# Fused attention and two expert layers on one core: the second raw copy and the gate rows of each head move forward, and 16 products of the first expert move ahead of its last columns

## The chip, the cores and the metric

The kernel runs on one core of a Trainium2 chip. The metric is the device time of one execution in microseconds (us), median over the runs. The kernel before was timed three times: 811.89, 816.52 and 813.16 us, median 813.16 us. The execution that the profiler recorded took 811.05 us.

## What is computed

Attention with a decaying causal mask over 4 batches of 8 heads, 576 positions and 64 channels a head, then two layers of experts on the 2304 rows that come out:

```python
scores = scale * np.matmul(q, k.transpose(0, 1, 3, 2))
cum = np.cumsum(np.log(np.clip(f, 0.0001, 1.0)), axis=-1)
scores = np.where(causal, -1e9, scores + cum[..., :, None] - cum[..., None, :])
attn = np.exp(scores - scores.max(-1, keepdims=True))
attn = attn / (attn.sum(-1, keepdims=True) + 1e-9)
x = (attn @ v).transpose(0, 2, 1, 3).reshape(2304, 512)
...
# layer 1: each row goes to the expert of its largest normalised logit
out[mask] = gate_w[mask, None] * (np.maximum(x[mask] @ w1[e], 0) @ w2[e])
...
# layer 2: each expert takes exactly 288 rows, in the order of the logits
out[mask] = np.maximum(x[mask] @ w1[e], 0) @ w2[e]
```

There are 8 experts in each layer, with 1024 hidden columns.

## The kernel before, in words

The 32 heads (4 batches by 8) are worked off in 32 slots; one slot takes some 7 us in the trace. Everything in a slot is written in a fixed order by hand, and each engine carries out its own instructions in that order, so an instruction that waits holds all that stands behind it on its engine. Products are kept at float32 precision by splitting each operand into a rounded high part and the remainder.

For head n there are two operand tiles: `opA` (the high parts, with rows for the mask, the row maximum and the gate sums below them) and `opB` (the remainders, crosswise). Three buffers of each go round, so slot n prepares head n+2 in the buffers that head n-1 has used. A preparation has these pieces:

- `load(n + 3)`: the raw q and k of a head that is one further on come from memory into `raw` (L307), and every second time v transposed into `vt` (L314). `load2(n + 2)`: two rows of gate sums go from `chl` into rows 64 and 65 of `opA` (L462, 2.2 KB each) and v by rows into `vv` (L463). All of these are asked for on the queue of SP.
- `prep(n + 2)` (L465) has two halves, t = 0 for q and t = 1 for k. Each half is a ScalarE (ACT) copy of `raw` into `opA` (L469), a GpSimd (POOL) subtraction that gives the remainder in `opB` (L470), and a request on SP that copies the high part across to the other half of `opB` (L471). Half 0 is issued at step 0 of the slot and half 1 at step 4.

The slot has six steps, the loop over i in L743. Step i issues one pair of score products of head n on TensorE (PE) with their exponentials on ACT (`st_steps`, L544 to L546, into PSUM tiles `px`), one product for the row maxima of head n+1 (`max_steps`, L508, into two PSUM tiles `pl`, reduced on VectorE (DVE) in L512 and L516), and some of the products of head n-1 with v (`av_steps`, L577). At i = 3 POOL splits the maxima (`rows1`, L523). After the six steps PE transposes the maxima (`rows`, L528), ACT puts them into `opA` (L529), and the first two maxima products of head n+2 are issued, mixed with the remaining products of L577. The first of those is the first reader of half 1 of the preparation and of the gate rows:

```python
nc.tensor.matmul(p[:, :wp], af[0:96, q0:q0 + 128], a[0:96, 1, k0:k0 + wp], start=True, stop=True)
```

Behind the last slot the routing of the rows to experts is computed, mostly on DVE, while PE already works on the first expert with the 256 rows that were known early: 96 products of 256 columns, 12 for each of 8 pieces of the hidden layer (`First.products`, L967). `fill(n)` issues the next n of them, and the seven numbers in `FILL` say how many go where. The last 112 rows of this expert come by an indirect transfer into `tail` (L947); `First.columns` turns them (four transposes on PE in L883, copies on ACT in L886, remainders on DVE in L887). Pieces 6 and 7 use the fourth part of the weights, whose high part `whi` is made on ACT and whose remainder `wlo` is made on DVE by `split(3)` (L812, then L857 and L863), behind the ordering of the experts (`order_all`, L162). Then `Experts.run` goes on with the last rows (L1567).

```python
first_expert.fill(FILL[3] - FILL[6])
first_expert.rest()
first_expert.fill(FILL[5])
first_expert.columns()
first_expert.fill(96 - sum(FILL[:4]) - FILL[5])
```

`rest` (L985) issues six subtractions on POOL (L990).

Of the kernel before, what the change touches and what calls it, by code (L numbers as in the profile page):

```python
# [25 lines left out]
N = B * S  # L26
# [12 lines left out]
AHEAD = (4, 5)  # L39
LATE = (0, 1, 2, 3)  # L40
BESIDE = (0, 0, 0, 0, 1, 2, 3, 2, 2)
FILL = (11, 9, 16, 36, 4, 0, 12)
EARLY = 256

TAILS1 = {0: (0, 0), 1: (1, 0), 2: (2, 0), 3: (2, 64), 4: (3, 0), 5: (3, 64), 6: (3, 96)}
# [6 lines left out]
def r32(ap):  # L52
    return ap.bitcast(F32)
# [236 lines left out]
def attention(tc, ctx, qkT, vrow, vT, f, emb, x_d, identf, identb, psum, R, tau, first_expert):  # L290


    nc = tc.nc
# [23 lines left out]
    def load(n):  # L317
        load_raw(n)
        load_vt(n)
# [17 lines left out]
    low = const.tile([128, 1], F32, name="low")  # L337
    nc.gpsimd.iota(low, pattern=[[0, 1]], base=64, channel_multiplier=-1, allow_small_or_imprecise_dtypes=True)

    NB = 3  # L340
# [4 lines left out]
    Ab, Bb = ([t[:, 0:2 * S].rearrange("p (t s) -> p t s", t=2) for t in ts] for ts in (Af, Bf))  # L345
# [5 lines left out]
    chl = const.tile([B * H, 2, S], F32R, name="chl")  # L351
# [5 lines left out]
    def ln(t):  # L357
        nc.scalar.activation(t, t, AF.Ln)
# [40 lines left out]
    def weights_of(k):  # L399


        t = R.room(k, [128, NCH * S + 64], F32)
        pt = t[:, 0:NCH * S].rearrange("p (j s) -> p j s", j=NCH)
        nc.gpsimd.memset(pt[:, 1:, 0:64], 1.0)
        nc.gpsimd.memset(t[:, NCH * S:], 1.0)
        nc.gpsimd.memset(pt[64:128, NCH - 1, S - 64:], 0.0)
        return t, pt
# [48 lines left out]
        for k in range(2):  # L456
            nc.vector.tensor_tensor(ENB[:, :, k + 1], ENB[:, :, k], half(ENB[:, :, k]), op=ALU.subtract)

    def load2(n):
        b, h = divmod(n, H)  # L460
        for i in range(2 if n > 1 else 0):
            nc.sync.dma_start(r32(Ab[n % NB][64 + i:65 + i, 1, :]), r32(chl[n:n + 1, i, :]))  # L462
        nc.sync.dma_start(Vb[n % 4][:, :, 0:D], vrow[b, h])  # L463

    def prep(n):  # L465
        a, b_, raw = Ab[n % NB], Bb[n % NB], RAW.pop(n)

        def half(t, hi, lo):
            nc.scalar.activation(a[0:64, t, :], raw[:, t, :], AF.Copy)  # L469
            nc.gpsimd.tensor_tensor(b_[lo, t, :], raw[:, t, :], r32(a[0:64, t, :]), op=ALU.subtract)  # L470
            nc.sync.dma_start(r32(b_[hi, t, :]), r32(a[0:64, t, :]))  # L471
        top, low = slice(0, 64), slice(64, 128)
        return [lambda: half(0, low, top), lambda: half(1, top, low)]

    def parts(n):

        v, r = VT[n][:, 0:S], cum0[:, n // 2 % 2, 0:S]
        (nc.vector if n else nc.gpsimd).tensor_tensor(r, v, half(v), op=ALU.subtract)
        yield
        (nc.gpsimd if n > 2 else nc.vector).tensor_tensor(half(r, 0), r, half(r), op=ALU.subtract)  # L480
# [39 lines left out]
    def rows1(n):  # L520

        mx = MB[n % 2][:, :, 48:49]
        nc.gpsimd.tensor_tensor(half(mx, 0), mx, half(mx), op=ALU.subtract)  # L523
# [7 lines left out]
    def st_steps(n):  # L531
        a, b_, af, bf = Ab[n % NB], Bb[n % NB], Af[n % NB], Bf[n % NB]
        pt = PT[n % 2][1]
        out = []
        for j, q0, q1 in ((0, 0, 288), (0, 288, 576), (1, 128, 576), (2, 256, 576), (3, 384, 576),
                          (4, 512, 576)):
            def step(j=j, q0=q0, q1=q1):
                kw = min(128, S - j * 128)
                k0 = j * 128
                w = q1 - q0  # L540
                wp = w if w <= 64 else max(w, 256)
                p = psum.tile([128, 512], F32, name="px", bufs=3)
                o, ks = p[:, 512 - wp:], slice(S + k0, S + k0 + 128)
                nc.tensor.matmul(o, af[:, ks], a[:, 0, q1 - wp:q1], start=True, stop=False)  # L544
                nc.tensor.matmul(o, bf[:, ks], b_[:, 0, q1 - wp:q1], start=False, stop=True)
                nc.scalar.activation(pt[:kw, j, q0:q1], p[:kw, 512 - w:], AF.Exp, scale=0.125)  # L546
                if j in (1, 3):
                    fl = pt.rearrange("p j s -> p (j s)")
                    d = bass.AP(tensor=fl.tensor, offset=fl.offset + (j - 1) * (S + 128),
                                ap=[fl.ap[0], [S + 128, 2], [1, 128]])  # L550
                    nc.gpsimd.affine_select(d, d, pattern=[[0, 2], [1, 128]], compare_op=ALU.is_ge,
                                            fill=0.0, base=0, channel_multiplier=-1)
                elif j == 4:
                    nc.gpsimd.affine_select(pt[:64, 4, 512:576], pt[:64, 4, 512:576],
                                            pattern=[[1, 64]], compare_op=ALU.is_ge,
                                            fill=0.0, base=0, channel_multiplier=-1)
            out.append(step)
        return out
# [3 lines left out]
    def av_steps(n):  # L562
        b, h = divmod(n, H)
        v_ = Vb[n % 4]
        p = AV[n % 2]
        if h == 0 and b not in X:
            X[b] = (work.tile([128, NCH, DM], F32, name="xr"),
                    work.tile([128, NCH, E, H], F32, name="lh"))
        out = []
        seen = []  # L570
        for i in AORD:
            j = seen.count(i)
            seen.append(i)

            def step(i=i, j=j, k=len(seen) - 1):
                c = j * S + i * 128
                nc.tensor.matmul(p[:, i, :], PT[n % 2][0][:, c:c + 128], v_[:, j, :], start=(k == 0),  # L577
                                 stop=(k == len(AORD) - 1))
            out.append(step)
        return out  # L580
# [110 lines left out]
    N = B * H  # L691
    for s in prep(0):
        s()
    second()
    pads()
    PT = [weights_of("hh")]
    load2(0)
    load2(1)
    ln(fr)
    h1 = prep(1)  # L700
    un = unit()
    next(un)
# [24 lines left out]
    def emit(l, k):  # L727
        for _ in range(k):
            if l:
                l.pop(0)()  # L730
    fin = iter(())
    pa = []
    for n in range(N):
        if n + 3 < N:
            load(n + 3)
        if n + 2 < N:
            load2(n + 2)
        pp = prep(n + 2) if n + 2 < N else []
        ss = st_steps(n)
        aa = av_steps(n - 1) if n else []  # L740
        if n % 2 == 0 and n + 2 < N:
            pa.append(parts(n + 2))
        for i in range(6):  # L743
            emit(ss, 1)
            emit(ms, 1)
            if n == 0 and i == 2:
                unit_columns()
            if n == 0 and i == 5:
                warm(nc, psum, identb, START[4], "px", 3)
            if i == (3 if n else 5) and n + 1 < N:  # L750
                rows1(n + 1)
                next(p0, None)
            if i in (0, 4):
                emit(pp, 1)
            emit(aa, APAT[i])
            if i in (1, 2):
                next(fin, None)
            if i in VPAT[min(n, 2 + n % 2)]:
                advance(pa, 1)
            if i in NPAT:  # L760
                advance(now, 1)
            if i in QPAT:
                advance(sq or slow, 1)
            if i in FPAT:
                advance(first3, 1)
            if i == 3:
                store()
        if n + 1 < N:
            rows(n + 1)
        ms = max_steps(n + 2) if n + 2 < N else []  # L770
        emit(ms, 1)
        emit(aa, 1)
        emit(ms, 1)
        emit(aa, 15)
        if (n % 2 or not n) and n + 1 < N:
            ven(n + n % 2)
        if n == 0:
            warm(nc, psum, identb, START[5], "px", 3)
        if n:
            fin = av_fin(n - 1)  # L780
            next(fin)
        if n == 1:
            now.append(setup())
# [7 lines left out]
    first_expert.W.upper(0, 2)  # L791
    first_expert.fill(FILL[0])
    for _ in av_fin(N - 1):
# [3 lines left out]
    for _ in range(2):  # L797
        first_expert.load_next()
    first_expert.fill(FILL[1])
    advance(sq, FILL[4])  # L800
    advance(now, 100)
    R.total = carry[0]
    first_expert.fill(FILL[2])
    u = R.tokens(psum, "px", 3, NC1, *R.one_hots)
# [8 lines left out]
    first_expert.load_next()  # L813
    first_expert.fill(FILL[6])
    advance(sq, 100)
    first_expert.fill(FILL[3] - FILL[6])
    first_expert.rest()
# [7 lines left out]
N = B * S  # L825
# [13 lines left out]
class Weights:  # L839
# [13 lines left out]
    def upper(self, key, j):  # L853
        pool, k, bufs = (self.pool, "1", 4) if j < 4 else (self.pool2, "2", 8)
        hi = pool.tile([128, 1024], F32R, name="whi" + k, bufs=bufs)
        lo = pool.tile([128, 1024], F32R, name="wlo" + k, bufs=bufs)
        self.nc.scalar.activation(hi, self.raw[key, j], AF.Copy)  # L857
        self.parts[key, j] = (hi, lo)

    def lower(self, key, j):  # L860

        hi, lo = self.parts[key, j]
        self.nc.vector.tensor_tensor(lo, self.raw.pop((key, j)), r32(hi), op=ALU.subtract)  # L863
# [1033 lines left out]
```

## Time and profile before

| what | before |
| --- | --- |
| median of three runs | 813.16 us |
| the profiled execution | 811.05 us |
| its span in the profile | 809.3 us |
| PE busy with products, share of the span | 741.2 us, 92% |
| PE busy with weight loads | 707.5 us, 87% |
| DVE busy | 500.6 us, 62% |
| ACT busy | 408.6 us, 50% |
| POOL busy | 302.6 us, 37% |

The span is the time from the first to the last instruction that the profiler recorded; the execution's own time is 1.75 us longer. Times in the rows further down are counted from the span's start. Slot 0 begins at about 29.5 us and the last slot ends at about 257 us; the first expert's last columns fall at about 271 us.

### The profile page before, as it was taken

How to read it: one execution, taken by the hardware profiler on the slowest of the kernel's cores; microseconds unless marked ns; L12 is line 12 of the kernel's file. 1: busy time of each engine (PE TensorE's matmuls, PEld its weight loads, DVE VectorE, ACT ScalarE, POOL GpSimd, SP SyncE). 2: the span in 40 equal slices, each digit the busy share in tenths (PEclk: the TensorE clock that was granted, in tenths of full speed). 3: DMA queues.
4: the chain of work that ended last, by engine and by line, in shares of the span. 5: the costliest groups of instructions: out<-in, count | busy, mean ns of one | idle time of the engine just before them, and what ended most of it. 6: DMA issues, size and time to landing. Idle time of an engine off the chain costs nothing. (4 is left out here: it accounts for less than half of the span.)

```text
span 809.3 us, 16361 instructions
## 1 busy us (share of the span) xinstructions
PE 741.2 (92%) x5813; PEld 707.5 (87%) x5813; DVE 500.6 (62%) x1314; ACT 408.6 (50%) x898; POOL 302.6 (37%) x674
## 2 busy tenths in 40 slices
PE   3799999999999899999999999925799999999995
PEld 1499999999989899999999999822799999999993
DVE  5766786787786777465465567674555655555530
ACT  3455666666756645455465567100555545555420
POOL 5676767676661635621222111003012322232011
PEclk9999999999999999999999999855899999999998
DMA  5455656566545456555566663004556656665310
GB/s 123 95 131 140 164 134 173 143 151 154 153 114 199 142 182 215 169 177 163 163 174 201 196 184 108 16 12 152 178 176 187 205 181 197 208 187 180 125 36 30
DMA packets 70255, 121.75 MB, mean 150 GB/s; under 512 B 29498, under 2 KB 38714, under 8 KB 70164
## 3 DMA queue, kind: packets, MB, share of 16 engines
q1 hardware_dynamic: 63924, 101.24, 44.3%
q0 software_dynamic: 6240, 19.36, 6.4%
q8 instruction: 50, 0.82, 0.4%
q14 instruction: 41, 0.34, 0.1%
HBM read 96.46 MB, written 14.63 MB: 137 GB/s over the span
## 5 line engine op out<-in xcount | busy, mean ns | idle before, releaser
L863 DVE TENSOR_TENSOR wlo<-wraw,whi 128x1024 fp32r<-128x1024 f32 x128 | 156.4, 1227 | 126.3 <-ACT whi L857 122.0
L857 ACT ACTIVATE whi<-wraw 128x1024 fp32r<-128x1024 f32 x128 | 134.6, 1056 | 4.3 <-DMA wraw<-v 3.5
L470 POOL TENSOR_TENSOR opB<-raw,opA 64x576 fp32r<-64x576 f32 x64 | 90.5, 1415 | 44.2 <-ACT opA L469 38.1
L1570 ACT ACTIVATE room_hh<-pl 128x288 fp32r<-128x288 f32 (+8 forms) x128 | 51.9, 406 | 96.9 <-PE pl L1567 96.4
L1567 PE MATMUL pl<-room_xh,whi 128*128 128x288 f32 (+7 forms) x512 | 94.7, 307 | 4.6 <-DVE room_hl L1571 4.4
L1567 PE MATMUL pl<-room_xl,whi 128*128 128x288 f32 (+7 forms) x512 | 90.5, 299 | 0.0
L1567 PE MATMUL pl<-room_xh,wlo 128*128 128x288 f32 (+7 forms) x512 | 90.0, 298 | 0.0
L1591 PE MATMUL py<-room_hh,wlo 128*128 128x288 f32 (+7 forms) x480 | 89.8, 311 | 0.0
L1571 DVE SCALAR_TENSOR_TENSOR room_hl<-pl,room_hh 128x288 fp32r<-128x288 f32 (+8 forms) x128 | 57.2, 448 | 50.5 <-ACT room_hh L1570 50.2
L1567 PEld LDWEIGHTS pl<-room_xh,whi 128*128 128x128 f32 x512 | 76.0, 191 | 6.3 <-DVE room_hl L1571 5.9
L508 PE MATMUL pl<-opA 96*128 96x288 f32 (+2 forms) x192 | 67.8, 358 | 11.2 <-DVE opA L382 4.4
L1567 PEld LDWEIGHTS pl<-room_xl,whi 128*128 128x128 f32 x512 | 76.7, 191 | 0.1
L1567 PEld LDWEIGHTS pl<-room_xh,wlo 128*128 128x128 f32 x512 | 76.2, 190 | 0.0
L1591 PE MATMUL py<-room_hh,whi 128*128 128x288 f32 (+7 forms) x480 | 76.0, 301 | 0.0
L1591 PE MATMUL py<-room_hl,whi 128*128 128x288 f32 (+7 forms) x480 | 75.8, 300 | 0.0
L1799 POOL DMA_INDIRECT xg<-y_d,ix x24 | 29.2, 1215 | 123.4 <-PE px L1507 88.5
L544 PE MATMUL px<-opA 128*128 128x288 f32 (+2 forms) x192 | 71.8, 374 | 0.1
L1591 PEld LDWEIGHTS py<-room_hh,wlo 128*128 128x128 f32 x480 | 70.6, 190 | 0.0
L577 PE MATMUL py<-vv,room_hh 128*128 128x73 f32 x480 | 69.8, 265 | 0.4 <-DVE vv L492 0.4
L512 DVE CUSTOM_DVE_ANT_0 mxs<-pl,mask 128x512 f32<-128x512 f32 (+3 forms) x128 | 61.9, 484 | 12.6 <-PE pl L508 9.1
L1591 PEld LDWEIGHTS py<-room_hh,whi 128*128 128x128 f32 x480 | 69.1, 189 | 0.0
L1591 PEld LDWEIGHTS py<-room_hl,whi 128*128 128x128 f32 x480 | 69.0, 189 | 0.0
(367 smaller groups left out, 1410.8 us busy)
## 6 DMA issues: line engine op xcount, KB each, us to landing
wraw<-w SPq DMA_DIRECT2D x64, 512.0 KB, 3.6
wraw<-v SPq DMA_DIRECT2D x64, 512.0 KB, 3.5
raw<-qkT SPq DMA_DIRECT2D x32, 288.0 KB, 4.1
opB<-opA SPq DMA_DIRECT2D x64, 144.0 KB, 2.7
vv<-vrow SPq DMA_DIRECT2D x32, 160.0 KB, 3.3
vt<-vT SPq DMA_DIRECT2D x16, 288.0 KB, 4.4
x_d<-xr SPq DMA_DIRECT2D x16, 256.0 KB, 3.2
opA<-chl SPq DMA_DIRECT2D x60, 2.2 KB, 3.4
```

What stands on the lines that cost most here:

```text
L470: nc.gpsimd.tensor_tensor(b_[lo, t, :], raw[:, t, :], r32(a[0:64, t, :]), op=ALU.subtract)
L508: nc.tensor.matmul(p[:, :wp], af[0:96, q0:q0 + 128], a[0:96, 1, k0:k0 + wp], start=True, stop=True)
L512: nc.vector.tensor_tensor_reduce(t[:qw, :w], p[:qw, :w], mask[:qw, m0:m0 + w], 1.0, part4[:qw] if i == 4 else -3.0e38, op0=ALU.add, op1=AL ...
L544: nc.tensor.matmul(o, af[:, ks], a[:, 0, q1 - wp:q1], start=True, stop=False)
L577: nc.tensor.matmul(p[:, i, :], PT[n % 2][0][:, c:c + 128], v_[:, j, :], start=(k == 0), stop=(k == len(AORD) - 1))
L857: self.nc.scalar.activation(hi, self.raw[key, j], AF.Copy)
L863: self.nc.vector.tensor_tensor(lo, self.raw.pop((key, j)), r32(hi), op=ALU.subtract)
L1567: nc.tensor.matmul(o, a[:, d, f0:f0 + 128], b[:, d, o0:C], start=(n == 0), stop=(n == 11))
L1570: nc.scalar.activation(hh[:, fc, c0:C], o, AF.Relu)
L1571: nc.vector.scalar_tensor_tensor(hl[:, fc, c0:C], o, 0.0, r32(hh[:, fc, c0:C]), op0=ALU.max, op1=ALU.subtract)
L1591: nc.tensor.matmul(o, a[:, fc, :], b[:, fc, :C], start=(n == 0), stop=(n == 23))
L1799: nc.gpsimd.indirect_dma_start(out=g[:w], out_offset=None, in_=y_d, in_offset=IOA(ap=ix2[:w, p * NT + t:p * NT + t + 1], axis=0))
```

## The change

It does three things. `prep` returns three pieces in place of two, and they are issued at steps 0, 2 and 4: ACT's second copy and the request on SP that follows it go to step 2, POOL's second subtraction stays at step 4. The two gate rows are asked for first in a slot, ahead of `raw` and `vt`. And `FILL[5]` goes from 0 to 16, so that 16 of the last 24 products of the first expert's early rows stand ahead of the transposes of its last rows, and 8 behind.

```diff
-FILL = (11, 9, 16, 36, 4, 0, 12)
+FILL = (11, 9, 16, 36, 4, 16, 12)
...
-    def load2(n):
+    def load_gates(n):
+        for i in range(2):
+            nc.sync.dma_start(r32(Ab[n % NB][64 + i:65 + i, 1, :]), r32(chl[n:n + 1, i, :]))
+
+    def load_v(n):
         b, h = divmod(n, H)
-        for i in range(2 if n > 1 else 0):
-            nc.sync.dma_start(r32(Ab[n % NB][64 + i:65 + i, 1, :]), r32(chl[n:n + 1, i, :]))
         nc.sync.dma_start(Vb[n % 4][:, :, 0:D], vrow[b, h])
 
     def prep(n):
         a, b_, raw = Ab[n % NB], Bb[n % NB], RAW.pop(n)
 
-        def half(t, hi, lo):
+        top, low = slice(0, 64), slice(64, 128)
+
+        def upper(t, hi):
             nc.scalar.activation(a[0:64, t, :], raw[:, t, :], AF.Copy)
+            nc.sync.dma_start(r32(b_[hi, t, :]), r32(a[0:64, t, :]))
+
+        def lower(t, lo):
             nc.gpsimd.tensor_tensor(b_[lo, t, :], raw[:, t, :], r32(a[0:64, t, :]), op=ALU.subtract)
-            nc.sync.dma_start(r32(b_[hi, t, :]), r32(a[0:64, t, :]))
-        top, low = slice(0, 64), slice(64, 128)
-        return [lambda: half(0, low, top), lambda: half(1, top, low)]
+        return [lambda: (upper(0, low), lower(0, top)), lambda: upper(1, top), lambda: lower(1, low)]
...
     for n in range(N):
+        if n + 2 < N:
+            load_gates(n + 2)
         if n + 3 < N:
             load(n + 3)
         if n + 2 < N:
-            load2(n + 2)
+            load_v(n + 2)
...
-            if i in (0, 4):
+            if i in (0, 2, 4):
                 emit(pp, 1)
```

Before the first slot, `load2(0)` and `load2(1)` become `load_v(0)` and `load_v(1)`, which ask for the same. The instructions are the same ones before and after; lines behind the edit carry other numbers (L469 becomes L473, L546 becomes L551, L529 becomes L534, L967 becomes L974).

ACT, one slot of the attention, before (`raw` into `opA` is the copy, `px` into `room_hh` is an exponential, `pr` into `opA` the maxima):

```order
L546 ACTIVATE room_hh<-px 128x288
L469 ACTIVATE opA_108<-raw 64x576
L546 ACTIVATE room_hh<-px 128x288
L546 ACTIVATE room_hh<-px 128x448
L546 ACTIVATE room_hh<-px 128x320
L546 ACTIVATE room_hh<-px 128x192
L469 ACTIVATE opA_108<-raw 64x576
L546 ACTIVATE room_hh<-px 64x64
L529 ACTIVATE opA_107<-pr 2x576
```

and now:

```order
L551 ACTIVATE room_hh<-px 128x288
L473 ACTIVATE opA_108<-raw 64x576
L551 ACTIVATE room_hh<-px 128x288
L551 ACTIVATE room_hh<-px 128x448
L473 ACTIVATE opA_108<-raw 64x576
L551 ACTIVATE room_hh<-px 128x320
L551 ACTIVATE room_hh<-px 128x192
L551 ACTIVATE room_hh<-px 64x64
L534 ACTIVATE opA_107<-pr 2x576
```

The second copy has passed the fourth and the fifth exponential; nothing else on ACT has moved.

SP's queue over one slot with a store, before (`opA<-chl` are the gate rows, `opB<-opA` the two crosswise copies, `x_d` the store of finished rows):

```order
L307 DMA raw<-qkT 64x2x576
L314 DMA vt_88<-vT 128x576
L462 DMA opA_106<-chl 1x16x36 x2
L463 DMA vv_113<-vrow 128x5x64
L471 DMA opB_109<-opA_106 64x576
L619 DMA x_d<-xr 128x4x128
L620 DMA x_d<-xr 64x128
L471 DMA opB_109<-opA_106 64x576
```

and now:

```order
L461 DMA opA_106<-chl 1x16x36 x2
L307 DMA raw<-qkT 64x2x576
L314 DMA vt_88<-vT 128x576
L465 DMA vv_113<-vrow 128x5x64
L474 DMA opB_109<-opA_106 64x576 x2
L624 DMA x_d<-xr 128x4x128
L625 DMA x_d<-xr 64x128
```

The gate rows have passed `raw` and `vt`, and the second crosswise copy has passed the store.

PE, the end of the first expert's early rows, before, with what each waits for (`whi_3937` and `wlo_3938` are the fourth part of the weights):

```order
L883 MATMUL px<-identf,tail 128x112 [waits DMASW2_49,PE_49]
L883 MATMUL px<-identf,tail 128x112 [waits PE_49]
L883 MATMUL py<-identf,tail 128x112 x2
L967 MATMUL pl<-room_xh,whi_3937 128x256 [waits Activation_49]
L967 MATMUL pl<-room_xh,whi_3937 128x256 x3
L967 MATMUL pl<-room_xl,whi_3937 128x256 x4
L967 MATMUL pl<-room_xh,wlo_3938 128x256 [waits DVE_49]
L967 MATMUL pl<-room_xh,wlo_3938 128x256 x3
L967 MATMUL pl<-room_xh,whi_3937 128x256 [waits Activation_49]
L967 MATMUL pl<-room_xh,whi_3937 128x256 x3
```

and now:

```order
L974 MATMUL pl<-room_xh,whi_3937 128x256 [waits Activation_49]
L974 MATMUL pl<-room_xh,whi_3937 128x256 x3
L974 MATMUL pl<-room_xl,whi_3937 128x256 x4
L974 MATMUL pl<-room_xh,wlo_3938 128x256 [waits DVE_49]
L974 MATMUL pl<-room_xh,wlo_3938 128x256 x3
L974 MATMUL pl<-room_xh,whi_3937 128x256 [waits Activation_49]
L974 MATMUL pl<-room_xh,whi_3937 128x256 x3
L890 MATMUL px<-identf,tail 128x112 [waits DMASW2_49,PE_49]
L890 MATMUL px<-identf,tail 128x112 [waits PE_49]
L890 MATMUL py<-identf,tail 128x112 x2
```

Sixteen products have passed the four transposes, among them the ninth, which waits for DVE's `wlo`.

## Rows read from the trace of the kernel before

**Rows 1.** The page, part 1: busy us (share of the span) x instructions.

```profile
PE 741.2 (92%) x5813; PEld 707.5 (87%) x5813; DVE 500.6 (62%) x1314; ACT 408.6 (50%) x898; POOL 302.6 (37%) x674
```

**Rows 2.** Slots 37.2:247.7; length, PE, PEld, DVE, ACT, POOL busy, clock, DMA share, GB/s.

```profile
37.20:247.70 210.50, 203.65 (x1845) 194.61 (x1843) 157.36 (x593) 131.12 (x336) 145.06 (x220) 1.00 0.58 149
```

**Rows 3.** Maxima products L508: what ended idle time before them (us in total, times).

```profile
  ACT opA L469: 6.1, 22
...
  ACT room_hl L546: 1.9, 4
...
  DMA opA<-chl: 1.8, 3
```

**Rows 4.** Timeline, PE: ends of four slots (start us, us, instruction [idle before <- releaser]).

```profile
56.73 0.45 PE L528 MATMUL pr<-identb,mb 128*128 128x128 bf16 x5 [0.19 <-POOL mb L523]
56.99 0.38 PE L508 MATMUL pl<-opA 96*128 96x288 f32 x1
...
70.95 0.19 PEld L508 LDWEIGHTS pl<-opA 96*128 96x128 f32 x1 [0.66 <-ACT room_hl L546]
...
126.42 0.44 PE L528 MATMUL pr<-identb,mb 128*128 128x128 bf16 x5
126.99 0.37 PE L508 MATMUL pl<-opA 96*128 96x288 f32 x1
...
141.17 0.19 PEld L508 LDWEIGHTS pl<-opA 96*128 96x128 f32 x1 [0.96 <-ACT lp L671]
```

**Rows 5.** Timeline, ACT: one slot's exponentials and copies.

```profile
126.00 0.33 ACT L546 ACTIVATE room_hl<-px 128x192 f32<-128x192 f32 x1 [0.53 <-PE px L545]
126.23 0.67 ACT L469 ACTIVATE opA<-raw 64x576 fp32r<-64x576 f32 x1
129.48 0.67 ACT L469 ACTIVATE opA<-raw 64x576 fp32r<-64x576 f32 x1
```

**Rows 6.** SP's requests at a slot's head; then part 6, median us from issue to landing.

```profile
120.95 0.66 SPq L307 DMA_DIRECT2D raw<-qkT  x1
122.33 1.18 SPq L462 DMA_DIRECT2D opA<-chl  x2
...
raw<-qkT SPq DMA_DIRECT2D x32, 288.0 KB, 4.1
opA<-chl SPq DMA_DIRECT2D x60, 2.2 KB, 3.4
```

**Rows 7.** A small DVE addition, by form; POOL and PE where one runs; a steady slot's DVE.

```profile
L223 DVE TENSOR_TENSOR pl_carry<-base,pl_carry x1: 1310/1310/1310, 106.5 to 106.5; 128x8 f32<-128x8 f32 x1
L223 DVE TENSOR_TENSOR pl_carry<-o_key,pl_carry x1: 154/154/154, 261.1 to 261.1; 128x8 f32<-128x8 f32 x1
...
106.37 1.40 POOL L470 TENSOR_TENSOR opB<-raw,opA 64x576 fp32r<-64x576 f32 x1
...
108.21 0.19 PEld L508 LDWEIGHTS pl<-opA 96*128 96x128 f32 x1 [0.47 <-DVE mx L516]
...
134.36 0.45 DVE L516 TENSOR_REDUCE mx<-pl 64x1 f32<-64x288 f32 x1 [0.96 <-PE pl L508]
```

**Rows 8.** Timeline, PE, ACT and DVE around the first expert's last columns.

```profile
266.99 0.63 PE L967 MATMUL pl<-room_xh,wlo 128*128 128x256 f32 x4
270.74 0.38 PE L883 MATMUL px<-identf,tail 112*128 112x112 f32 x2 [3.13 <-DMA tail<-x_d,gix]
271.09 0.72 PE L967 MATMUL pl<-room_xh,whi 128*128 128x256 f32 x4
...
273.97 0.64 PE L1567 MATMUL pl<-room_xh,whi 128*128 128x256 f32 x4
...
267.41 0.38 ACT L973 ACTIVATE both<-pl 128x256 f32<-128x256 f32 x1
...
269.70 1.62 DVE L863 TENSOR_TENSOR wlo<-wraw,whi 128x1024 fp32r<-128x1024 f32 x1
271.74 0.45 DVE L887 TENSOR_TENSOR room_xl<-py,room_xh 128x112 fp32r<-128x112 f32 x2
```

More of the change, by code (lines that the diff above doesn't have):

```diff
@@ L696, in attention @@
     PT = [weights_of("hh")]
-    load2(0)
-    load2(1)
+    load_v(0)
+    load_v(1)
     ln(fr)
```

## Prediction

> **What bounds the kernel now.** I read the page first: products keep PE busy for 92% of the span, the next engine reaches 62% [rows 1]. A change is worth what it takes off PE's idle time, or what it adds there. Next the busy times in one stretch of the slots: of 210.5 us PE is at products for 203.65, at the full granted clock of 1.00 (the 2.4 GHz level), while ACT is busy for 131 us and DVE for 157 [rows 2]. So about 7 us are idle on PE, in 30 slots. Then the waits of the maxima products, where nearly all of this lies: 22 times the first maxima product at a slot's end waited for ACT's raw copy, 6.1 us in total; four more times it waited for the gate rows or something that ended at the same moment [rows 3]. The timeline shows how one looks. In a slot where nothing is late, this product starts 0.26 us after the first transpose of the maxima (56.73 to 56.99); in a slot that waits it starts 0.57 us after it (126.42 to 126.99) [rows 4]. ACT's second copy began only at 126.23, behind the fifth exponential, and ended at 126.90, so its end is what released the product [rows 5]. In the four other slots the weight load stood idle for 0.66 us (the first of them, at 70.95) to 0.96 us (the last, at 141.17) [rows 4], and PE for 1.8 us in three of them until the gate rows had landed [rows 3].
>
> **The copy at step 2.** The instruction is the same, 0.67 us on ACT [rows 5]. At step 2 it stands ahead of the fourth exponential, and that one had ended by 125.47 in this slot (126.00 less the 0.53 us that ACT idled [rows 5]); so the copy is done more than 1 us ahead of its reader, and the 6.1 us of the 22 waits go. It needs no new data: it reads `raw`, which half 0 has read two steps earlier, and half 1 of `opA`, whose last reader was the slot before. What it passes is two exponentials. The fourth can be up to 0.67 us late; the fifth waits 0.53 us for PE today [rows 5], which takes up most of that. Both leave their `px` tile to a score product three pairs later, in the next slot, so PE does not see it. I cost it at nothing; without that slack it would be at most 0.67 - 0.53 = 0.14 us a slot, 4 us in 30 slots. Behind the step, the last exponential and the maxima's copy L529 come earlier by up to 0.67 us, and PE's next scores wait for the latter.
>
> The request on SP for the crosswise copy moves with it, ahead of the store; its result is read two slots later. POOL's second subtraction stays at step 4 and can start once the mask of the fifth exponential is done, a little sooner than now, where it also waits for the copy.
>
> **The gate rows first.** Their requests take 1.18 us for two and stand behind `raw` (0.66 us) and, every second slot, `vt` [rows 6]. They move ahead by at least 0.66 us, and SP also comes to them sooner, since the crosswise copy that it waited for is done at step 2. They land 3.4 us after the request in the median [rows 6]. That covers the four waits: the weight load idled 1.9 us there by ACT's row, less 0.2 us that is PE's own, and 1.0 us in the slot at 141.17 [rows 3, 4]; together **2.6 us**. `raw` now stands behind 1.18 us of gate requests, and those wait for the last score product of the slot before. It is asked for at 120.95 and first copied at 129.48, 8.5 us later, and lands in 4.1 us [rows 5, 6]; so 4.4 us of cover remain, and I cost it at nothing.
>
> Together the waits are 6.1 + 2.6 = **8.7 us**. From start to start a gap shrinks by 0.57 - 0.26 = 0.31 us, which in 22 slots is 6.8 us instead of 6.1, so 9.4 us at most. Not all of it is gain: in three slots (at 108.21 and twice more with the same routing step) PE waits at the next maxima product for DVE, 0.47 us [rows 7]. If PE arrives 0.26 us sooner there, it only waits longer. I take 0.5 us off and 0.2 for a late L529 in slots with squares on ACT: **8.0 us**, between 7.0 and 9.4.
>
> What holds DVE up in those three slots can be read: its addition of 128x8 elements lasts 1.31 us there, with POOL's subtraction running from 106.37 to 107.77, and 0.154 us where POOL is idle [rows 7]. The Trainium skill (SBUF — State Buffer, section "SBUF: two separate sides") says that POOL and a VectorE operation with two SBUF inputs share a port pair that one of them holds for its whole instruction; the trace agrees, with 1.31 against 0.154 us. By that rule the three slots are freed as soon as POOL's earlier subtraction ends, and the 0.5 us come back; without it they stay lost.
>
> **The 16 products.** Today PE ends the 72nd product at 267.62 and stands idle for 3.13 us until `tail` lands; then come four transposes and 24 products, from 271.09 to 273.97, 0.12 us each [rows 8]. Sixteen products are 1.9 us and would fit into the gap. But the ninth to twelfth of them read `wlo`, and DVE has that done only at 269.70 + 1.62 = 271.32 [rows 8], later than `tail`. So: the first starts at 267.79, when ACT has emptied the PSUM tile; eight run until 268.75; PE waits for DVE until 271.32; eight more until 272.28; the transposes, now behind them, 0.35 us, until 272.63; the last eight until 273.59. Against 273.97 that is **0.4 us** gained where 1.9 us were to be had. The remainders of the columns end 1.45 us after the first transpose now (270.74 to 272.19) [rows 8], so about 273.75, and the group of products that reads them begins at 274.07: just in time. Bounds: 1.9 us gained if `wlo` came early, 0.8 us lost if the columns were waited for in full.
>
> **The sum.** 8.0 + 0.4 = 8.4 us. Behind these places PE goes on with the experts without a wait that ends on anything but PE's own progress, so I let the whole of it arrive at the end: the profiled execution of 811.05 us would take 802.7. That execution is 2.1 us below the median of the three runs, 813.16; from the median the forecast is **804.8 us**, 1.0% faster. Its own range is 803 to 806.5.
>
> **Rivals.**
>
> 1. *The gate rows take the place of the copy.* They land 3.4 us after the request, the last time asked for at about 122.9 and so there at 126.3, against the product at 126.96 [rows 4, 6]: they were only some 0.6 us ahead. If requests on SP do not really move (because the store, or the wait for PE's last score, now holds them), half of the 8.7 us stays: 813.2 - 4.0 - 0.4 = 808.8 us. Against it: SP is free at the slot's head earlier, and `raw` alone stood for 0.66 us in front.
>
> 2. *The gain is absorbed later.* PE comes sooner to the first expert, but the ordering on DVE, or the weights, are not sooner. Then the wait for `wlo` grows by what was gained: 811 to 813 us, no change. Against it: DVE's routing there starts from the last head's result, which PE delivers sooner.
>
> 3. *Slower: POOL's earlier subtraction holds up DVE.* An addition on DVE stretches from 0.154 to 1.31 us while POOL subtracts [rows 7]. If DVE had an operation with two SBUF inputs queued between the last maxima of a slot and the first ones of the next in every slot, as it has in the three, each slot would get the 0.47 us wait at the next maxima product: 28 x 0.47 = 13.2 us lost against 8.4 gained, 818 us. It decides where DVE has less than about 0.5 us of slack; in a steady slot it waits 0.96 us for PE ahead of this reduction [rows 7], which speaks against it. The Trainium skill (SBUF — State Buffer, section "SBUF: two separate sides") gives the rule by which this would come about: whichever of the two starts first keeps the port pair to its end.
>
> **How the numbers follow.** A measurement of this kernel can tell about 0.5% (4.1 us) from no change. Forecast: 0.74. Rival 1: 0.14, half of it below 809.1. Rival 2: 0.08. Rival 3, or `raw` landing more than its 4.4 us late, 0.04. So faster 0.81, within 0.5% 0.15, slower 0.04. The range reaches down to 802, for all 9.4 us, 0.4 and a run like the profiled one, and up to 809.5, to take in rival 1.
>
> **What would show it.** Right: in the profile after, the rows that name ACT's raw copy and `opA<-chl` as releasers of the maxima products are gone or below 1 us, the product follows the first transpose by 0.26 us in nearly all slots, and PE's idle time ahead of the first expert's last columns has moved in front of a product that reads `wlo`, named as released by DVE, with 2 to 3 us. Wrong: waits on `opA<-chl` of several us (rival 1), a DVE wait longer by the same amount behind the slots (rival 2), or L516 as a releaser in most slots (rival 3).

## The result, and the profile after

The changed kernel takes **805.86 us** in the median of four runs (804.62 to 806.44); beside it the kernel before takes 814.71 us (811.89 to 816.52). The ratio is 0.9892, with a 95% interval of 0.9856 to 0.9928. So it is faster by 8.9 us, where 8.4 was forecast (804.8 us). The profiled execution took 805.88 us, its span is 803.7 us. Behind the diff's added lines all line numbers are higher: L469 is L473, L470 L477, L508 L513, L516 L521, L523 L528, L528 L533, L863 L870, L883 L890, L967 L974, L1567 L1574.

Part 1 of the page hardly moves against [rows 1]:

```profile
PE 741.7 (92%) x5813; PEld 711.0 (88%) x5813; DVE 498.0 (62%) x1314; ACT 408.3 (51%) x898; POOL 303.3 (38%) x674
```

The gain shows in the stretch of the slots, cut at the same product in both kernels: from slot 1's first maxima product to slot 29's. First the kernel before, then the changed one (length, PE, PEld, DVE, ACT, POOL busy, clock, DMA share, GB/s):

```profile
43.36:240.12 196.76, 190.37 (x1725) 182.00 (x1725) 147.44 (x560) 123.86 (x319) 137.08 (x209) 1.00 0.59 149
```

```profile
43.95:231.70 187.75, 184.68 (x1728) 180.96 (x1726) 145.63 (x560) 123.23 (x318) 137.56 (x210) 1.00 0.67 155
```

The same work takes 196.76 - 187.75 = **9.0 us** less, at a clock of 1.00 in both. What ended the idle time before the maxima products in the changed kernel (us in total, times):

```profile
  DVE mx L521: 7.1, 10
...
  DVE mb L517: 1.4, 2
```

ACT's raw copy (6.1 us, 22 times) and the gate rows of [rows 3] are gone without rest. The end of a slot, PE's timeline, to be set beside [rows 4]:

```profile
123.37 0.44 PE L533 MATMUL pr<-identb,mb 128*128 128x128 bf16 x5
123.62 0.38 PE L513 MATMUL pl<-opA 96*128 96x288 f32 x1
...
105.87 0.19 PEld L513 LDWEIGHTS pl<-opA 96*128 96x128 f32 x1 [0.76 <-DVE mx L521]
```

The product follows the transpose by 0.25 to 0.27 us in the last 30 slots; before it was 0.52 us or more in 26 of these. The last row is the weight load that waited 0.47 us for DVE in [rows 7]: it waits longer now, as it does in the other two routing slots.

The first expert's last columns, PE and DVE, beside [rows 8]:

```profile
258.58 0.63 PE L974 MATMUL pl<-room_xh,wlo 128*128 128x256 f32 x4
259.44 0.74 PE L974 MATMUL pl<-room_xh,whi 128*128 128x256 f32 x4 [0.23 <-ACT both L980]
263.00 0.74 PE L974 MATMUL pl<-room_xh,wlo 128*128 128x256 f32 x4 [2.35 <-DVE wlo L870]
264.04 0.36 PE L890 MATMUL px<-identf,tail 112*128 112x112 f32 x2
265.43 1.05 PE L974 MATMUL pl<-room_xh,wlo 128*128 128x256 f32 x4
266.28 1.05 PE L1574 MATMUL pl<-room_xh,whi 128*128 128x256 f32 x4
...
261.29 1.65 DVE L870 TENSOR_TENSOR wlo<-wraw,whi 128x1024 fp32r<-128x1024 f32 x1
```

The idle time has moved in front of the ninth product and is named as a wait for `wlo`, as forecast. But from the start of the last four of the first 72 products to the first product of the next stage (the **tail** from here on) it is 266.28 - 258.58 = 7.70 us, against 273.97 - 266.99 = 6.98 before: 0.7 us lost where 0.4 us gained was forecast. A group of four products lasts 1.05 us where it lasted 0.63. The page's windows say why (columns as above):

```profile
260.00:264.00 4.00, 1.65 (x14) 1.44 (x13) 2.87 (x4) 0.23 (x1) 2.36 (x8) 1.00 0.07 23
264.00:268.00 4.00, 4.00 (x24) 4.00 (x23) 2.22 (x8) 1.27 (x6) 0.00 (x0) 0.57 0.37 130
```

After two idle stretches on PE close together (0.23 and 2.35 us) the granted clock had a mean of 0.57 in these 4 us: for most of them it was at the 1.2 GHz level.

The two profiled executions differ by 5.6 us in span, which splits thus: slots -9.0; tail +0.7; the start up to slot 1 +0.6 (43.36 to 43.95); from the next stage's first product to the end +2.1 (535.3 to 537.4 us), of which 0.6 is the low clock behind the tail and 1.5 the second routing and the products behind it, which the change doesn't touch. The medians differ by more, 8.9 us. One reason is on record: the profiled execution of the kernel before, 811.05 us, is below all 25 others that were timed (811.89 to 818.84 us), while that of the changed kernel lies at its median.

### The profile page after: what moved, and what is told of

It is laid out like the page before. It is cut to its first block, busy times and chain, and to the rows that moved or that the text cites. A ratio compares the mean times of both kernels' runs of the same rounds, so it can differ in the third digit from the quotient of the medians.

```text
span 803.7 us, 16338 instructions
## 1 busy us (share of the span) xinstructions
PE 741.7 (92%) x5813; PEld 711.0 (88%) x5813; DVE 498.0 (62%) x1314; ACT 408.3 (51%) x898; POOL 303.3 (38%) x674
## 5 line engine op out<-in xcount | busy, mean ns | idle before, releaser
L870 DVE TENSOR_TENSOR wlo<-wraw,whi 128x1024 fp32r<-128x1024 f32 x128 | 156.3, 1227 | 126.4 <-ACT whi L864 122.0
L477 POOL TENSOR_TENSOR opB<-raw,opA 64x576 fp32r<-64x576 f32 x64 | 90.7, 1417 | 34.3 <-ACT opA L473 31.6
L1574 PE MATMUL pl<-room_xh,whi 128*128 128x288 f32 (+7 forms) x512 | 94.9, 308 | 4.5 <-DVE room_hl L1578 4.4
L1574 PE MATMUL pl<-room_xl,whi 128*128 128x288 f32 (+7 forms) x512 | 90.6, 299 | 0.0
L1574 PE MATMUL pl<-room_xh,wlo 128*128 128x288 f32 (+7 forms) x512 | 90.5, 299 | 0.0
L1574 PEld LDWEIGHTS pl<-room_xh,whi 128*128 128x128 f32 x512 | 76.4, 192 | 6.1 <-DVE room_hl L1578 5.6
L1574 PEld LDWEIGHTS pl<-room_xl,whi 128*128 128x128 f32 x512 | 76.8, 191 | 0.0
L1574 PEld LDWEIGHTS pl<-room_xh,wlo 128*128 128x128 f32 x512 | 76.7, 191 | 0.0
L513 PE MATMUL pl<-opA 96*128 96x288 f32 (+2 forms) x192 | 67.5, 356 | 7.0 <-DVE opA L382 3.7
```

The costliest lines, as they stand in the source:

```text
L1574: nc.tensor.matmul(o, a[:, d, f0:f0 + 128], b[:, d, o0:C], start=(n == 0), stop=(n == 11))
```

## Experiments

Twelve runs follow, of nine other kernels and the changed one again, in three groups, each group on one chip with the kernel before beside it; the tail and the stretch of slots are read from each kernel's profile.

**Each part alone.** First the 16 products on the kernel before:

```
-FILL = (11, 9, 16, 36, 4, 0, 12)
+FILL = (11, 9, 16, 36, 4, 16, 12)
```

> The kernel before with FILL[5] = 16 alone. Two stretches are read from each profile: the slots, from the first maxima product at the end of slot 1 to the one at the end of slot 29 (196.8 us before, 187.8 after the whole change), and the tail, from the start of the last four of the first 72 early products to the first product of Experts.run (6.98 us before, 7.70 after). Theory: the 16 products do not gain, they stop at the ninth until DVE has written wlo, and after that idle time PE's granted clock falls (0.57 from 264 to 268 us in the profile after), so the tail is 7.4 to 8.0 us, the slots stay at 196.8 and the time is 0 to 2 us above the kernel before. Rival, the forecast's term: the low clock there was chance; the tail is 6.6 us with the clock at 1.00 and the time 0.4 us below.

814.85 us, ratio 0.9998 (0.9959 to 1.0037). The slots are nearly as before, 240.48 - 44.15 = 196.33 us; the tail is 274.19 - 267.35 = 6.84 us, so the 16 gain 0.14 us:

```profile
267.35 0.62 PE L967 MATMUL pl<-room_xh,wlo 128*128 128x256 f32 x4
271.80 0.74 PE L967 MATMUL pl<-room_xh,wlo 128*128 128x256 f32 x4 [2.38 <-DVE wlo L863]
272.85 0.36 PE L883 MATMUL px<-identf,tail 112*128 112x112 f32 x2
274.19 0.64 PE L1567 MATMUL pl<-room_xh,whi 128*128 128x256 f32 x4
```

Then the change without them:

```
-FILL = (11, 9, 16, 36, 4, 16, 12)
+FILL = (11, 9, 16, 36, 4, 0, 12)
```

> The whole change without the 16 products (FILL[5] = 0). Theory: the slots are 187.8 us as after the whole change, the tail is 6.98 us with the clock at 1.00 as before, and the time is 9 to 10 us below the kernel before, 0 to 2 us below the whole change. Rival: the 16 products bring 0.4 us; then this kernel is 0.4 us slower than the whole change. A third reading: the low clock comes from the faster slots and not from the 16 products; then the clock falls in the tail here too.

803.20 us, ratio 0.9858 (0.9822 to 0.9893), some 11 us below the kernel before; slots 230.60 - 42.88 = 187.72 us. So all of the gain is in the attention; the profiles show 9.0 us of it in the slots and 0.6 us in the tail. The tail is 6.39 us and not 6.98 as before, with the same order of work:

```profile
257.48 0.62 PE L974 MATMUL pl<-room_xh,wlo 128*128 128x256 f32 x4
260.02 0.38 PE L890 MATMUL px<-identf,tail 112*128 112x112 f32 x2 [1.92 <-DMA tail<-x_d,gix]
261.88 0.74 PE L974 MATMUL pl<-room_xh,wlo 128*128 128x256 f32 x4 [0.34 <-DVE wlo L870]
263.87 0.64 PE L1574 MATMUL pl<-room_xh,whi 128*128 128x256 f32 x4
```

The gathered rows came sooner: 5.1 us after their request by part 6, against 6.3 us before (6.4 with the 16 products on the kernel before). The transposes now run while `wlo` is being written, and only 0.34 us of wait for `wlo` is left.

Of the two edits in the attention, the copy alone (gate requests behind `raw` and `vt` again, no 16 products):

```
     for n in range(N):
-        if n + 2 < N:
-            load_gates(n + 2)
         if n + 3 < N:
             load(n + 3)
         if n + 2 < N:
+            load_gates(n + 2)
             load_v(n + 2)
```

> Only the copy at step 2; the gate rows are asked for behind raw and vt as before, and FILL[5] = 0. Theory by the terms of the sum: the 6.1 us of waits for the copy go, the 2.6 us for the gate rows stay; the slots are 189.5 to 191 us. Rival: the copy alone also frees SP earlier, so that the gate rows come in time wherever they stand in the queue; then the slots are 187.8 us and no product waits for opA<-chl.

803.93 us, ratio 0.9868 (0.9834 to 0.9902); slots 232.23 - 44.54 = 187.69 us, every product 0.25 to 0.27 us behind its transpose. The gate rows come in time without having been moved. SP's timeline shows the cause: the requests of the crosswise copy wait for ACT's copy, and SP's queue with them. Two of them in the kernel before (the requests behind them are in [rows 6]), then two here with what follows, and the end of the same slot on PE:

```profile
116.72 4.14 SPq L471 DMA_DIRECT2D opB<-opA  x2
```

```profile
114.48 2.53 SPq L474 DMA_DIRECT2D opB<-opA  x2
117.10 0.66 SPq L307 DMA_DIRECT2D raw<-qkT  x1
...
118.49 1.18 SPq L461 DMA_DIRECT2D opA<-chl  x2
...
123.95 0.44 PE L533 MATMUL pr<-identb,mb 128*128 128x128 bf16 x5
124.21 0.38 PE L513 MATMUL pl<-opA 96*128 96x288 f32 x1
```

4.14 us became 2.53, so the queue gets to the gate rows sooner against the same product: 5.7 us ahead of it here (118.49 against 124.21), 4.7 before (122.33 against 126.99 [rows 4, 6]). In the four slots that had waited for the gate rows, the second of the two requests stood 4.3 to 4.7 us ahead of the product before, and stands 5.0 to 5.1 us ahead of it here. And the gate rows first alone (the copy back at step 4, no 16 products):

```
-        return [lambda: (upper(0, low), lower(0, top)), lambda: upper(1, top), lambda: lower(1, low)]
+        return [lambda: (upper(0, low), lower(0, top)), lambda: (upper(1, top), lower(1, low))]
...
-            if i in (0, 2, 4):
+            if i in (0, 4):
```

> Only the gate rows asked for first; the copy stays at step 4, and FILL[5] = 0. Theory: the four waits for the gate rows go down to the 0.3 us of the 22 others, so 1.5 us of the 2.6 are gained and 26 waits for the copy are left (about 7.5 us); the slots are about 195.2 us, the time 1 to 2 us below the kernel before, hardly to be told from it. Rival: raw behind the gate rows comes late; then ACT's first copy waits for raw and the slots are longer than 196.8 us.

814.21 us, ratio 0.9987 (0.9952 to 1.0021), no difference that these runs tell; slots 242.31 - 46.78 = 195.53 us, 1.2 us less than before. The gate rows are gone as a releaser, but all 26 slots now wait for the copy:

```profile
  ACT opA L473: 7.2, 26
```

**What the 16 products wait for.** Half of them, those that read no `wlo`:

```
-FILL = (11, 9, 16, 36, 4, 16, 12)
+FILL = (11, 9, 16, 36, 4, 8, 12)
```

> The change with 8 instead of 16 products of the first expert ahead of the last columns: whi times room_xh and room_xl, the eight that need no wlo. Theory (the ninth product's wait for wlo is what the 16 lose; the eight ahead of it run in time in which TensorE had nothing): from the start of the last four of the first 72 products to the first product of the next stage 6.2 to 6.4 us, against 7.70 in the change and 6.39 with none ahead; time 803.5, some 1.5 to 2 below the change on the same chip and within 0.5 of the one with none ahead. Rival (the 16 cost nothing and the change's tail was long for the low granted clock there, which comes and goes by itself): the same time as the change within 0.5 us.

805.36 us, ratio 0.9874 (0.9853 to 0.9896): nearer to the rival, 0.6 us under the change on the same chip. The tail is 265.17 - 258.00 = 7.17 us, above the forecast of 6.2 to 6.4. PE stands idle three times (0.24, 0.67 and then 1.12 us for `wlo`), and the clock falls behind them, to a mean of 0.68 from 262 to 266 us:

```profile
262.43 0.73 PE L974 MATMUL pl<-room_xh,wlo 128*128 128x256 f32 x4 [1.12 <-DVE wlo L870]
263.47 1.05 PE L974 MATMUL pl<-room_xl,whi 128*128 128x256 f32 x4
264.32 1.05 PE L974 MATMUL pl<-room_xh,wlo 128*128 128x256 f32 x4
...
262.00:266.00 4.00, 3.57 (x20) 3.57 (x21) 1.70 (x7) 0.77 (x2) 0.00 (x0) 0.68 0.43 131
```

Two groups took 0.85 us from start to start instead of 0.47: without that the tail would be 7.17 - 2 x 0.38 = 6.41 us, what it is with none ahead. So the eight bring nothing either: `wlo` sets the end.

If that is so, the 16 are worth something once `wlo` is early:

```
+    first_expert.split(3)
     for _ in R.order_all():
         pass
     first_expert.last_rows(work)
-    first_expert.split(3)
```

> The change with the last split of the first weights (ScalarE's whi and VectorE's wlo of its fourth piece) put ahead of the steps that sort the experts, so that wlo is written sooner. Theory: the wait of 2.35 us at the ninth of the 16 products goes; the stretch from the last four of the first 72 products to the next stage falls from 7.70 to 5.1 to 5.5 us, and the granted clock does not fall behind it; time 802.5 to 803.5. Rival (what the columns wait for is the late thing, not wlo): the wait moves from the ninth product to the transposes or to the first product of the next stage, and the stretch stays above 6.3 us.

802.04 us, ratio 0.9844 (0.9819 to 0.9869). `wlo` is written ahead of the ordering of the experts, and the wait is gone; the tail is 262.88 - 258.34 = **4.54 us**, less than the 5.1 to 5.5 expected, with the clock at 1.00. On the same chip the change took 805.97 us, so 3.9 us are gained, 2.3 of them in the tail (against 6.80 us there):

```profile
256.54 1.22 DVE L870 TENSOR_TENSOR wlo<-wraw,whi 128x1024 fp32r<-128x1024 f32 x1
...
258.34 0.63 PE L974 MATMUL pl<-room_xh,wlo 128*128 128x256 f32 x4
260.24 0.63 PE L974 MATMUL pl<-room_xh,wlo 128*128 128x256 f32 x4
262.88 0.72 PE L1574 MATMUL pl<-room_xh,whi 128*128 128x256 f32 x4 [0.20 <-DVE room_hl L984]
```

The same with none of the 16 ahead (`FILL[5]` 0):

> As the one before, with none of the 16 products ahead of the last columns. Theory: without them the transposes wait for the gathered rows and the products behind them for the copied columns, so the stretch is 6.0 to 6.4 us, as with the late split; the 16 are then worth 0.7 to 1.2 us, which is what they were worth apart from wlo. Rival (the early split by itself brings all): stretch and time as in the run with the 16, within 0.3 us.

803.45 us, ratio 0.9861 (0.9837 to 0.9886); tail 264.96 - 258.70 = 6.26 us, as the theory had it. With `wlo` early the 16 are worth 6.26 - 4.54 = 1.7 us, nearly the 1.9 us that they last; with `wlo` late they are worth nothing. The times, 802.04 and 803.45 us, go the same way, though the intervals of their ratios overlap.

The change itself once more:

> The change itself once more, as the measure of the other three on the same chip, and to see whether the granted clock of 0.57 behind its last columns comes again. Theory (it follows from the two idle stretches around the 16 products): wait of 2.3 to 2.4 us at the ninth product again, clock again near 0.57 in the four us behind it, stretch 7.7 us, time 805 to 806.5. Rival (the low clock was a chance of that execution): clock at 1.00 there, stretch 6.8 to 7.0 us.

805.97 us, ratio 0.9896 (0.9871 to 0.9922). The wait for `wlo` is 2.35 us again, but the tail is 266.54 - 259.74 = 6.80 us, and the clock behind it 1.00. Here the theory missed: the low clock in the tail is not the rule.

```profile
264.00:268.00 4.00, 3.85 (x33) 3.85 (x34) 2.10 (x9) 1.50 (x6) 0.00 (x0) 1.00 0.36 131
```

**POOL beside DVE.** On the kernel with `wlo` early and the 16 products, POOL's second subtraction of a slot one step later:

```
-            if i in (0, 2, 4):
+            if i in (0, 2, 5):
```

> The run with the early split of the first weights, and in every slot of the attention POOL's second subtraction (raw minus opA into the low half, 1.4 us) one step later, at the sixth step instead of the fifth. Theory (in the three routing slots VectorE's tiny L223 takes 1.3 instead of 0.15 us since it lies beside that subtraction, and the maxima behind it let PEld wait 0.75 us): L223 falls to 0.15 to 0.25 us there, the three waits of 0.74 to 0.76 us go, and the stretch from slot 1 to slot 29 falls from 187.7 to 185.2 to 185.8 us; time 800 against 802.0. Rival (POOL's subtraction then runs into the next slot's first one, and POOL's masks of the products come 0.6 us late, or the long operation lies on the maxima instead): slots as long or longer, 187.7 to 192 us, with new waits of PE for POOL.

801.68 us (799.86 to 803.21), ratio 0.9817 (0.9791 to 0.9842), the lowest median of all, though the step alone is not told from the 802.04 us of the run it builds on. Slots 231.35 - 45.19 = 186.16 us, 1.5 less than the 187.71 of that run, where 1.9 to 2.5 were expected. The tail took 5.03 us instead of 4.54, where PE waited 0.66 us for the gathered rows, which took 6.2 us to land. DVE's small addition and the waits of PE's weight load between 45 and 232 us (us in total, times, longest):

```profile
105.38 0.15 DVE L223 TENSOR_TENSOR pl_carry<-base,pl_carry 128x8 f32<-128x8 f32 x1
...
PEld L533 <- POOL mb L528: 2.2, 3, 1.1
PEld pl L513 <- DVE mx L521: 0.7, 1, 0.7
```

In the changed kernel the same view has 3.1 us in four waits for `mx` and 1.2 us in two for `mb`. The three routing slots are free; 1.0 us came back as waits for POOL's split of the maxima (`mb`; 0.4 of it just ahead of the stretch), while the rival had named POOL's masks. One step sooner instead:

```
-            if i in (0, 2, 4):
+            if i in (0, 2, 3):
```

> As the one before, with that subtraction one step sooner, at the fourth step. Theory: it then lies beside VectorE's 0.75 us running sum instead of L223, so L223 is short and the three waits go, at the cost of a longer running sum; slots 185.2 to 186.5 us if the sum has room. Rival: POOL's mask behind it waits for it, and products that need the mask come late in every slot: over 187.7 us.

807.06 us, ratio 0.9892 (0.9873 to 0.9910): slots 236.26 - 45.33 = 190.93 us, the rival's side, though by another wait than it named. L223 is short, 0.16 us, as expected. But DVE's running sum beside the subtraction takes 1.30 us instead of 0.75, and with DVE late another operation of the routing (L240) comes to lie beside the next subtraction, with 1.68 us instead of 0.42. The maxima keep their own times and come late; most of the loss lies in four slots (12 and 13, 20 and 21: 7.48 and 6.81 or 6.82 us, against 6.65 and 6.25), not in every slot:

```profile
103.82 1.40 POOL L477 TENSOR_TENSOR opB<-raw,opA 64x576 fp32r<-64x576 f32 x1
...
115.40 1.42 POOL L477 TENSOR_TENSOR opB<-raw,opA 64x576 fp32r<-64x576 f32 x1 [1.67 <-ACT opA L473]
...
104.53 1.30 DVE L483 TENSOR_TENSOR cum<-vt 128x576 f32<-128x576 f32 x1
...
115.42 1.68 DVE L240 TENSOR_TENSOR ohl<-iotab,pl_ci 128x256 bf16<-128x256 bf16 x1
...
PEld pl L513 <- DVE mb L517: 2.8, 5, 0.8
PEld pl L513 <- DVE mx L521: 2.8, 7, 0.7
PEld L533 <- POOL mb L528: 1.7, 3, 0.7
```

**The change with and without its 16 products, on one chip.**

> The change without its 16 products once more, to stand beside the change on one chip. Theory (the 16 put two idle stretches where one was, and cost 0.4 us at the full clock and up to 1.5 us where the clock falls): stretch of the tail 6.4 us, clock at 1.00 there, and a time 1 to 2.7 us under the change's. Rival (the difference between the two so far was the chip's): within 0.5 us of the change.

> The change, on the chip of the three others. Theory: stretch of the tail 6.8 us at the full clock or 7.7 us with the clock near 0.57 behind its wait, time 805 to 807 and 1 to 2.7 us over the one without the 16 products. Rival: within 0.5 us of that one.

Without: 803.21 us, ratio 0.9843 (0.9823 to 0.9862), tail 265.03 - 258.65 = 6.38 us. With: 806.16 us, ratio 0.9888 (0.9857 to 0.9920), tail 267.10 - 260.29 = 6.81 us at a clock of 1.00. The medians differ by 2.95 us, a little above the theory's 2.7. The profiles put only 0.43 us of it in the tail. Of the 2.7 us between the two spans, 1.64 are there at slot 1 (44.06 against 45.70), ahead of anything that the 16 products touch, and go with the clock of the start (the stretch from 16 to 46 us; without, then with the 16):

```profile
16.00:46.00 30.00, 21.96 (x148) 15.37 (x149) 21.24 (x59) 12.35 (x28) 20.25 (x41) 0.84 0.40 92
```

```profile
16.00:46.00 30.00, 23.22 (x123) 15.73 (x123) 21.23 (x55) 12.21 (x28) 19.00 (x41) 0.72 0.42 94
```

The other 0.6 us lies behind the tail. Over all executions the change took 806.2 us in the mean (12, clock 0.949 to 0.959), without the 16 803.3 us (8, clock 0.957 to 0.965). At the same clock they lie nearer: at 0.957 four executions of 805.84 to 806.47 us against two of 804.16 and 805.17 us, at 0.959 four of 804.62 to 805.78 us against one of 803.75 us. So about half of the 3 us goes with the clock. That the 16 cost time is measured; that the tail alone costs it is shown for 0.4 us, and for 1.9 us (7.70 - 6.39, and 0.6 of low clock behind it) in the one profile where the clock fell. **What makes the rest is open.** The clock at the start may differ by chance: the program's order is the same up to there, and that stretch had 0.89 to 0.67 in the kernels without the 16 products too (0.67 with the gate rows first alone). Against it stands that the lower clock went with the 16 products over the twenty executions. It was not tested by itself.

## Why the prediction was right, point by point

**The copy at step 2: right, and it does more than was said.** The 22 waits went, and the products follow in 0.25 us. This one edit is enough for all 9.0 us of the slots (187.69 us with it alone). Rival 1's doubt whether SP's requests would move at all is answered: they do, but it is the copy that moves them.

**The gate rows first: the 2.6 us were about right as a size and wrong as to the cause.** Their terms, 1.9 - 0.2 + 1.0, add up to 2.7, and the gaps of the four slots shrank by 2.8 us. The step said that they "move ahead by at least 0.66 us, and SP also comes to them sooner, since the crosswise copy that it waited for is done at step 2". The second half alone suffices. The edit itself brings 1.2 us without the copy and nothing beside it (187.75 against 187.69 us). `raw` was not late in any slot.

**What was taken off, 0.7 us.** In the three routing slots the waits grew from 0.47 or 0.48 us to between 0.74 and 0.76 us, and so by 0.8 us together, where 0.5 was taken. No wait for L529 shows; another 0.3 us went to POOL's `mb` in the fourth slot (0.33 to 0.65 us). Yet 8.0 was forecast and 9.0 measured, inside the 7.0 to 9.4 given. Two terms were mis-sized. The 8.7 us of waits are 9.1 us as gaps from start to start: 6.3 in the slots that waited for the copy and 2.8 in the four others (9.4 with the gap just ahead of the stretch, the most that the text gave). And the 0.7 us of loss is 0.1 in the sum over the slots: three slots lost 0.6 us outside these gaps, and nearly as much came back in small amounts in the others, for reasons that no run shows.

Those slots' addition lasts 1.29 us beside POOL's subtraction and 0.15 us when the subtraction is moved off it. The Trainium skill (SBUF — State Buffer, section "SBUF: two separate sides") lets the engine that starts first hold the shared port pair for its whole instruction. The trace agrees, with 0.15 and 1.29 us. In the changed kernel:

```profile
104.02 1.41 POOL L477 TENSOR_TENSOR opB<-raw,opA 64x576 fp32r<-64x576 f32 x1
...
104.17 1.29 DVE L223 TENSOR_TENSOR pl_carry<-base,pl_carry 128x8 f32<-128x8 f32 x1
105.38 0.44 DVE L521 TENSOR_REDUCE mx<-pl 64x1 f32<-64x288 f32 x1
```

The prediction let that rule free the slots by itself, because the subtraction would start sooner, though its sum did not count on it; it did not start sooner against DVE's work. It begins 1.35 us ahead of the maxima before (106.37 and 107.72) and 1.36 us after, since it stands behind POOL's mask, which waits for an exponential. Rival 3 did not come about: DVE still has room, and waits for PE ahead of this reduction 22 times, 19.1 us in total. The subtraction one step sooner shows its mechanism, with 190.93 us.

**The 16 products: the wrong term.** 0.4 us gained was forecast; at the full clock 0.14 us are gained on the kernel before, and 0.4 us lost beside the rest of the change. The wait at the ninth product came where it was put and lasted 2.35 us. What failed is the comparison: the step set the new order against a tail in which PE stood 3.13 us for the gathered rows. With the change's attention the rows land 5.1 to 5.6 us after the request instead of 6.3, and the old order then runs the four transposes inside the wait for `wlo`; with the 16 ahead, they stand behind it. That is 0.6 of the 0.8 us between forecast and result (the old order takes 6.39 us and not 6.98). The other 0.2 is the new order's own tail, 6.81 us where the step's times give 6.60. Why the rows land sooner no run shows. The bound of 1.9 us gained "if `wlo` came early" was right, and the run with the early split gives 1.7 of it.

**The sum.** 8.0 + 0.4 was forecast. The profiles give 9.0 in the slots and, against the kernel before, -0.7 to +0.2 in the tail; the medians give 8.9 us. In the tail 0.6 us comes from the attention, which the prediction did not have, and the 16 products take 0.4 or more of it back. So the mechanism of the larger term was right, and that the total came out within 0.5 us is partly luck: errors of opposite sign, and one part of the medians' difference that no profile shows.

## What to carry to other kernels

A copy that one engine makes can hold a request queue for another's data: count what the queue holds up behind the wait, and the order of requests may not need changing at all. Before work is put into an idle stretch, ask which of the things awaited there comes last. Work that itself waits for the latest one only moves what would have run free behind that wait; here the same 16 products were worth nothing or 1.7 us, depending on when `wlo` was written. And price such an edit on the kernel that the other edits make, not on the one before.

## What the runs showed of the hardware

The same program, with the same two idle stretches on PE (0.23 or 0.24, and 2.35 or 2.36 us), went on behind them at a granted clock of 0.57 in one profile and 1.00 in two; 3.13 us in one piece in the kernel before left it at 1.00. Three idle stretches (0.24, 0.67 and 1.12 us), in the run with eight products ahead, were followed by 0.68. The gathered rows took 6.3 or 6.4 us from request to landing in the three kernels without the early copy, and 5.1 to 5.9 us in all of the others whose profile shows it but one (6.2 with POOL's subtraction last). A cast of eight numbers on DVE took 1.36 to 1.51 us beside POOL's six subtractions in the three profiles of the changed kernel, and 0.16 us behind them with `wlo` early; it is one of the steps that `wlo` stood behind. The two small gate requests landed in 3.4 and 3.2 us in the median where they stood behind `raw`, in 1.8 to 2.1 us ahead of it (not every landing is in the traces).
